# Moving a half's rows from the sync queue in place of the scalar queue, and the loads and logarithms of three batches with it

## The chip, the cores and the metric

The kernel runs on one core of a Trainium2 chip (trn2). The metric is device time in microseconds (us) from start to end of one execution. A core has five engines, each with its own queue of instructions that it takes in order: PE (TensorE, matrix products), DVE (VectorE), ACT (ScalarE), POOL (GpSimd) and SP (SyncE, which here only starts transfers). Sixteen DMA engines carry the transfers; SP, ACT and POOL can start them.

## The reference

Four batches of eight heads run a recurrence over 768 steps with a 40 x 40 state per head, and its output feeds a two-layer network with a squared ReLU:

```python
batch, n_heads, seq, head_dim = (4, 8, 768, 40)
for t in range(S):
    y[:, :, t] = np.einsum('bhd,bhde->bhe', rt, state)
    Sa = np.einsum('bhde,bhe->bhd', state, at)
    state_decay = state * wt[:, :, None, :] - np.einsum('bhd,bhe->bhde', Sa, bt)
    state = state_decay + np.einsum('bhd,bhe->bhde', vt, kt)
...
x = y.transpose(0, 2, 1, 3).reshape(3072, 320)
h = x @ w_in                # 320 x 2048
r = np.maximum(h, 0.0)
out = (r * r) @ w_out       # 2048 x 320
```

Inputs r, k, v, w, a, b are float32, as is the output of 3072 x 320.

## The kernel before

**Tiling.** Time is cut into 6 chunks of 128 steps. A chunk of one batch of the reference is what the code calls batch `m`, so there are 24 of them (`NBC`). Each holds 8 heads, two heads to a pair. The recurrence inside a chunk is turned into matrix products with decay factors taken from the cumulated logarithm of w. A stage `st` handles two pairs, half a batch: 48 stages (`NS`), 8 of them to a chunk (`NQ`). Batch `m` is worked in stages 2m and 2m + 1.

**One stage.** The loop over `st` (L635) lays the instructions of every engine out by hand, in the order in which each engine then runs them. For stage `st`, PE makes products `ca` (L329, for the next stage), `ex` (L436, for the stage before), `P` (L345, L351, L367). `P` is corrected twice: ACT copies it as `Mc` (L360), PE adds a product to it, DVE takes the difference `c` (L375), PE adds another product, and ACT writes the result, negated, into `EVX` (`st_sn`, L383; called Sn). Then come a transpose (L411, L422) and the products `uy` (L461), from which DVE makes the stage's rows of output, `YS` (L471). Between these, at marked places (`prepare(st, "P")`, `"C"`, `"A"`, `1`, `"S"`, `"T"`, `4`, `5`), steps for batches to come are put in, and at the calls of `filler` a piece of the network's work, or, before there is any, nine products for warmth (`warm`, L122).

**Preparing a batch.** `load` (L75) brings six arrays of 160 KB (W, K, A, B, V, R) from HBM, one transfer each, all started by SP. The buffers hold four batches. For batches from 4 on, a one-element write to W's new buffer (L80) stands ahead as a gate, on DVE for batches below 8 and on POOL from 8 on: SP does not start W's transfer until that engine has come to the place. `prep_ln` (L189) is the logarithm of W on ACT. `prep_all` (L206) is, for batches up to 7: PE's cumulated sum `cs` of it (L219), the exponentials `GI` (L226) and `GA` (L228) on ACT, and on POOL the scaled K and B (L238) and the copies of A, V and R (L285, L202). Two stages before their use follow the transposes (L246) and ACT's copies `GT` and `KBT` (L296, L263). For batches 8 and up the steps are spread over more places.

**Which step stands where** is a table, `plan`: an offset in stages from 2m, a place in the stage, and the function. For batches 1 to 7 the logarithm stands in stage 2m - 3 at place "T" and `prep_all` at place 5 of the same stage. At place "T" the stage's order is: Sn and what follows it on POOL, then `release()` (ACT's ReLU copies `hs`, L538, that are held back), a filler, and then the logarithm. Place "S" stands directly behind Sn and ahead of `release()`. Loads are let go at place 5, the last place of a stage, at offsets of their own.

**The network.** When four stages are through, half of a chunk's batches (`h`, called a half here; 12 in all) has its rows in `YS`. Two of the 40-row pieces of the fourth pair are moved to free rows of other pairs, so that the 320 rows fit three tiles: `gather` (L504), four transfers within SBUF of 12 and 8 KB. `feed` then queues the half's products as filler two stages later: `hp` (L527), `hs` (L538), its square `Gt` (L539, on POOL, every fourth on DVE), and `op` (L560) with the output's copy and store (L566, L568). For the first two halves (h = 0 behind stage 5, h = 1 behind stage 9) ACT starts the four transfers, for the others SP, and for the last SP and POOL. The call stands at the end of the stage, ahead of place 5.

Of the kernel before, what the change touches and what calls it, by code (L numbers as in the profile page):

```python
# [18 lines left out]
def kernel(  # L19
# [21 lines left out]
    nc = tc.nc  # L41

    NB, NHH, T, D = r.shape
# [5 lines left out]
    NS = NCH * NQ  # L49
# [5 lines left out]
    AHEAD, EARLY = 4, 7  # L55
# [266 lines left out]
    def st_a_mm(st):  # L322
        c, o, j0, p2, EVX = where(st)
        ca = CNs[st, "ps"] = [ps.tile([128, 2, 2, L], FP32, name=f"ca{s}", tag=f"ca{s}")
                              for s in range(2)]
        for u in range(2):
            for i in range(2):
                for s in range(2):
                    nc.tensor.matmul(out=ca[s][:, i, u, :], lhsT=o.KBT[half(s), u, j0 + i, :],  # L329
                                     rhs=o.AT[half(s), j0 + i, :], start=(i == 0 and u == 0),  # L330
                                     stop=True, skip_group_check=True)
# [7 lines left out]
    def st_p(st):  # L339
        c, o, j0, p2, EVX = where(st)  # L340
        CN, UZ = CNs[st], UZs[c % 2]
        P = Ps[st] = ps.tile([128, 2, 2, 64], FP32, name="P", tag="sp")
        if c > 0:
            for i in range(2):
                nc.tensor.matmul(  # L345
                    out=P[:, i, :, 0:D], lhsT=o.AT[:, j0 + i, :],
                    rhs=UZ[:, p2.start + i, :].rearrange("p (s d) -> p s d", s=2)[:, :, 0:D],
                    start=(i == 0), stop=False, skip_group_check=True)
        for i in range(2):
            for s in range(2):  # L350
                nc.tensor.matmul(out=P[:, i, s, 0:D], lhsT=CN[:, i, s, 0, :],  # L351
                                 rhs=EVX[:, i, s, L:LV], start=(c == 0 and i == 0 and s == 0),
                                 stop=False, skip_group_check=True)

    def st_m(st):
        c, q = divmod(st, NQ)
        if q == 0:
            Mc[c] = chp.tile([128, NQ, 4, D], BF16, name="Mc", tag="Mc")
            Cc[c] = chp.tile([128, NQ, 4, D], BF16, name="Cc", tag="Cc")
        nc.scalar.activation(out=Mc[c][:, q], func=ACTF.Copy,  # L360
                             in_=Ps[st][:].rearrange("p i s e -> p (i s) e")[:, :, 0:D])
# [28 lines left out]
    def st_jk(st, CN):  # L390
        jk = qdp.tile([128, 2, 2, L], BF16, name="jk", tag="jk", bufs=1)
        nc.scalar.activation(out=jk[:], in_=CN[:, :, :, 1, :], func=ACTF.Square,  # L392
                             accum_out=ACC[:, AN + st:AN + st + 1])
# [33 lines left out]
    def st_ex_mm(st):  # L427
        c, o, j0, p2, EVX = where(st)
        SnT = SnTs.pop(st)
        ex = exs[st] = [ps.tile([128, 2, 2, L], FP32, name=f"ex{s}", tag=f"ex{s}")  # L430
                        for s in range(2)]
        for u in range(2):
            for i in range(2):
                for s in range(2):
                    lhsT = SnT[half(s), i, :] if u else o.RVT[half(s), 1, j0 + i, 0:L]
                    nc.tensor.matmul(out=ex[s][:, i, u, :], lhsT=lhsT,  # L436
                                     rhs=o.RVT[half(s), 0, j0 + i, 0:L],
                                     start=(i == 0 and u == 0), stop=True, skip_group_check=True)

    def st_ex_ev(st, s):  # L440
        EVX = EVXs[st % NEV]
        nc.vector.tensor_tensor(  # L442
            out=EVX[:, :, s, 0:2 * LV].rearrange("p i (u x) -> p i u x", u=2)[:, :, :, 0:L],
            in0=exs[st][s][:], in1=MEX[:].rearrange("p (i u) x -> p i u x", u=2), op=ALU.mult)
# [21 lines left out]
    def st_y(st):  # L466
        c, o, j0, p2, EVX = where(st)
        uy = uys.pop(st)
        if st % NQ == 0:
            YSs[c] = chp.tile([128, NP, L], BF16, name="YS", tag="YS", bufs=3)  # L470
        nc.vector.tensor_tensor(out=YSs[c][:, p2, :], in0=uy[:, :, 0:L],  # L471
                                in1=o.GT[:, j0:j0 + 2, 0:L], op=ALU.mult)
        if c + 1 < NCH:
            nc.vector.tensor_tensor(
                out=UZs[(c + 1) % 2][:, p2, :].rearrange("p i (s d) -> p i s d", s=2)[:, :, :, 0:D],
                in0=uy[:, :, L:LV].rearrange("p i (s d) -> p i s d", s=1)
                .to_broadcast([128, 2, 2, D]),
                in1=o.GL[:, j0:j0 + 2, :].rearrange("p i (s d) -> p i s d", d=1)
                .to_broadcast([128, 2, 2, D]), op=ALU.mult)
# [21 lines left out]
    def by_pair(c, hf):  # L501
        return YSs[c][:].rearrange("e (b p) t -> e p b t", b=NB)[:, :, HB * hf:HB * hf + HB, :]

    def gather(c, hf, engines):  # L504
        X = by_pair(c, hf)
        for x, (p, row, h, e0, n) in enumerate(MOVED):
            src = 64 * (h % 2) + e0
            engines[x % len(engines)].dma_start(out=X[row:row + n, p], in_=X[src:src + n, h // 2])
# [3 lines left out]
    def release():  # L512
        while held:
            held.pop(0)()
# [82 lines left out]
    for m in range(1, NBC):  # L597
        if m <= EARLY:
            lot = "T" if m <= AHEAD else "S"
            plan = ((-3, "T", prep_ln), (-3, 5, prep_all), (-2, lot, prep_ga_mm),  # L600
                    (-2, lot, prep_ga_ev), (-2, lot, prep_kb), (-2, lot, prep_at))
        else:
            plan = ((-5, 5, prep_ln), (-4, "P" if m > EARLY + 1 else 5, prep_new),
                    (-4, 1, prep_sums), (-4, "S", prep_exps), (-4, 5, prep_scaled),
                    (-3, "C", prep_ga_mm), (-3, "C", prep_ga_ev), (-3, "A", prep_at),
                    (-3, "T", prep_kb), (-3, 4, prep_cast_rv), (-2, "P", prep_v))
        plan += ((-1, "T" if m == 1 else "C", prep_rv) if m <= AHEAD else
                 (-1, 1, prep_rv) if m < 2 * NB else (-2, 5, prep_turn),)
        if m >= AHEAD:
            plan += (({AHEAD: -9, AHEAD + 1: -8, EARLY: -6}.get(m, -7), 5, load),)  # L610
        for ds_, lot, f in plan:
            todo = when.setdefault((2 * m + ds_, lot), [])
            todo.insert(0 if f is prep_exps else len(todo), (f, m))

    def prepare(st, lot):
        for f, m in when.pop((st, lot), []):
            f(m)
# [17 lines left out]
    for st in range(NS + 2):  # L635
        late = st == 1
        if st + 1 < NS and not late:
            st_a_mm(st + 1)
        if 1 <= st <= NS:
            st_ex_mm(st - 1)  # L640
        if st < NS:
            st_p(st)
            st_m(st)
        if 1 <= st <= NS and st % 2:
            st_jk(st - 1, Ns.pop(st - 1))
        if st >= 2:
            st_y(st - 2)
        if 1 <= st <= NS:
            st_ex_ev(st - 1, 0)
        prepare(st, "P")  # L650
        filler(st)
        if 1 <= st <= NS and st % 2 == 0:
            st_jk(st - 1, Ns.pop(st - 1))
        if 1 <= st <= NS:
            st_z(st - 1)
        if st < NS:
            st_corr(st, Mc[st // NQ][:, st % NQ], False)
            st_c1(st)
        if late:
            st_a_mm(st + 1)  # L660
        st_energy(st - NQ // 2)
        prepare(st, "C")
        if 1 <= st <= NS:
            st_ex_ev(st - 1, 1)
        prepare(st, "A")
        if st + 1 < NS:
            st_a_ev(st + 1)
        filler(st, st % 2 == 0)
        prepare(st, 1)
        if st < NS:  # L670
            st_corr(st, c1s[st], True)
            Ns[st] = st_sn(st)
        prepare(st, "S")
        release()
        filler(st)
        prepare(st, "T")
        st_t(st, st - 2)
        flush()
        prepare(st, 4)
        if st >= NS - 4:  # L680
            filler(st)
        if 1 <= st <= NS:
            st_kb(st - 1)
        if 1 <= st <= NG:
            load_win(st - 1)
        if st == NQ - 1:
            load_wout()
        if st >= 2 and (st - 2) % (NQ // 2) == NQ // 2 - 1:
            h = (st - 2) // (NQ // 2)
            gather(*divmod(h, 2), [nc.scalar] if h < 2 else [nc.sync] if st < NS + 1 else  # L690
                   [nc.sync, nc.gpsimd, nc.sync])
            feed(st + 2, h)
        prepare(st, 5)

# [136 lines left out]
```

## Time and profile before

| | us |
|---|---|
| median of 3 runs | 292.8 |
| lowest, highest | 292.66, 294.53 |
| the profiled execution's own time | 291.61 |
| its span, first to last instruction | 289.8 |
| granted TensorE clock | 0.998 |

| engine | busy us | share of the span |
|---|---|---|
| PE | 264.9 | 91% |
| DVE | 210.0 | 72% |
| ACT | 207.0 | 71% |
| POOL | 214.8 | 74% |

The profile is of one execution. Times in it count from the span's start. A row of a timeline has the start, the duration, the engine, the line of the kernel, the operation, what it writes and reads, and how many such instructions are taken together; in square brackets stands the idle time of the engine just ahead of the row and what ended it. An engine's name with q behind it (SPq, ACTq) is its sequencer starting a transfer, which is not counted as busy time. By these rows stage 0 begins at about 11 us, stage 5 at about 36, stage 6 at about 41, stage 9 at about 58 and stage 10 at about 63.

### The profile page before, as it was taken

Reading aid. Unit: us, or ns where it says so; the run is one execution under the profiler, and the core shown is the slowest. Engines: PE = TensorE matmul, PEld = TensorE weight load, DVE = VectorE, ACT = ScalarE, POOL = GpSimd, SP = SyncE. Lnnn points to the kernel's source line nnn. Section 1 sums busy time; section 2 is a strip of 40 time slices with the busy share of each in tenths; the row PEclk is TensorE's granted clock in tenths of the full one; section 3 lists DMA queues with packets and bytes.
Section 4 is the critical chain, followed back from the end, with each engine's and each line's share of the span. In section 5 each row is a group of like instructions: output and inputs, shape, how many; then the busy total and the mean of one; then the engine's idle time right before and its main releaser. Section 6 shows DMA issues by size and latency. Waiting matters only on the chain.

```text
span 289.8 us, 10084 instructions
## 1 busy us (share of the span) xinstructions
PE 264.9 (91%) x3963; PEld 208.2 (72%) x3963; DVE 210.0 (72%) x461; ACT 207.0 (71%) x534; POOL 214.8 (74%) x414
## 2 busy tenths in 40 slices
PE   6878968987889999999999999999999999899892
PEld 5667757766568777877787787778777877666581
DVE  7568858775658789778888887898889787762140
ACT  4666557848586888888888878888887886746370
POOL 7889816858588988998998898889888988534400
PEclk9999999999999999999999999999999999999999
DMA  7999998794644976895989958959968923000001
GB/s 127 169 169 180 191 166 150 93 186 82 127 76 95 195 136 99 169 175 101 178 148 145 167 92 147 180 109 179 165 115 161 146 42 61 31 23 28 26 28 53
DMA packets 175351, 35.57 MB, mean 123 GB/s; under 512 B 169840, under 2 KB 174976, under 8 KB 175296
## 3 DMA queue, kind: packets, MB, share of 16 engines
q1 hardware_dynamic: 172224, 32.14, 63.3%
q0 software_dynamic: 2640, 2.63, 5.7%
q8 instruction: 33, 0.54, 0.8%
q14 instruction: 22, 0.18, 0.2%
q10 hardware_dynamic: 432, 0.08, 0.1%
HBM read 28.84 MB, written 3.93 MB: 113 GB/s over the span
## 4 chain that ended last, share of the span: by engine, by line
PE 72%; POOL 8%; ACT 6%; DMA 6%; issue 3%; SPq 2%; DVE 1%; POOLq 0%; DVEq 0%; ACTq 0%
PE hp L527 19%; PE tt L246 6%; PE ca L329 5%; PE cs L219 4%; PE uy L461 4%; PE ex L436 3%; POOL Gt L539 3%; PE P L367 3%; PE tb L411 3%; PE P L345 2%; PE wu L122 2%; DMA NR<-in_r_dram 2%; PE uy L451 2%; SPq L81 2%; ACT hs L538 2%
## 5 line engine op out<-in xcount | busy, mean ns | idle before, releaser
L539 POOL TENSOR_TENSOR Gt<-hs 128x512 bf16<-128x512 bf16 x66 | 68.0, 1043 | 24.9 <-ACT hs L538 24.8
L527 PE MATMUL hp<-YS,WIN 120*128 120x256 bf16 (+1 forms) x576 | 77.6, 272 | 0.5 <-ACT hs L538 0.4
L442 DVE TENSOR_TENSOR EVX<-ex,MEX 128x512 bf16<-128x512 f32 x96 | 65.4, 682 | 6.5 <-PE ex L436 6.0
L538 ACT ACTIVATE hs<-hp 128x512 bf16<-128x512 f32 x96 | 55.3, 602 | 15.9 <-PE hp L527 14.4
L337 DVE TENSOR_TENSOR CN<-ca,MCN 128x512 bf16<-128x512 f32 x96 | 61.4, 681 | 0.7 <-PE ca L329 0.7
L527 PEld LDWEIGHTS <-WIN 120*128 120x128 bf16 (+1 forms) x576 | 49.7, 97 | 6.9 <-issue 1.0
L560 PEld LDWEIGHTS <-Gt 128*128 128x128 bf16 x384 | 35.0, 97 | 13.4 <-POOL Gt L539 1.4
L375 DVE TENSOR_TENSOR c<-P,Mc 128x160 bf16<-128x160 f32 x48 | 15.6, 325 | 30.1 <-PE P L367 22.6
L367 PEld LDWEIGHTS <-CN 128*128 128x128 bf16 x384 | 22.2, 96 | 11.2 <-issue 7.7
L238 POOL TENSOR_TENSOR KBp<-NK,GI 128x320 bf16<-128x320 f32 x24 | 20.7, 863 | 12.8 <-ACT GI L226 12.2
L387 POOL TENSOR_TENSOR Cc<-x,EVX 128x160 bf16<-128x160 f32 x48 | 23.4, 487 | 8.9 <-ACT EVX L383 5.4
L392 ACT ACTIVATE jk<-CN 128x512 bf16<-128x512 bf16 x48 | 29.9, 623 | 0.0
L386 POOL TENSOR_TENSOR x<-Mc,c 128x160 f32<-128x160 bf16 x48 | 23.4, 487 | 7.0 <-DVE c L375 6.9
L422 DVE COPY TB<-tb 128x512 bf16<-128x512 bf16 (+1 forms) x48 | 19.3, 401 | 10.6 <-PE tb L417 7.7
L263 ACT ACTIVATE KBT<-tt 128x1024 bf16<-128x1024 bf16 x24 | 24.4, 1018 | 0.3 <-PE tt L246 0.3
L471 DVE TENSOR_TENSOR YS<-uy,GT 128x256 bf16<-128x256 f32 x48 | 19.9, 416 | 4.8 <-PE uy L461 4.8
L461 PE MATMUL uy<-EVX,KBp 128*64 128x168 bf16 x384 | 22.0, 236 | 0.0
L539 DVE TENSOR_TENSOR Gt<-hs 128x512 bf16<-128x512 bf16 x30 | 16.3, 543 | 7.2 <-ACT hs L538 7.2
L122 PE MATMUL wu<-ones_b 128*128 128x128 bf16 x265 | 20.4, 227 | 1.1 <-DVE ones_b L103 1.1
L329 PE MATMUL ca<-AT,KBT 64*128 64x128 bf16 x384 | 19.3, 219 | 2.0 <-ACT KBT L263 2.0
L383 ACT ACTIVATE EVX<-P 128x160 bf16<-128x160 f32 x48 | 14.4, 301 | 9.2 <-PE P L367 9.0
L360 ACT ACTIVATE Mc<-P 128x160 bf16<-128x160 f32 x48 | 14.6, 304 | 8.3 <-PE P L351 7.9
(138 smaller groups left out, 577.4 us busy)
## 6 DMA issues: line engine op xcount, KB each, us to landing
NW<-in_w_dram SPq DMA_DIRECT2D x24, 160.0 KB
NK<-in_k_dram SPq DMA_DIRECT2D x24, 160.0 KB, 4.0
NA<-in_a_dram SPq DMA_DIRECT2D x24, 160.0 KB
NB<-in_b_dram SPq DMA_DIRECT2D x24, 160.0 KB, 4.2
NV<-in_v_dram SPq DMA_DIRECT2D x24, 160.0 KB, 3.4
NR<-in_r_dram SPq DMA_DIRECT2D x24, 160.0 KB, 3.8
out_dram<-osb SPq DMA_DIRECT2D x24, 160.0 KB, 2.1
WOUT<-in_moe_w_out_dram POOLq DMA_DIRECT2D x1, 1280.0 KB, 11.2
```

Source lines behind the costliest of these rows:

```text
L122: nc.tensor.matmul(out=wu[:], lhsT=ones_b[:], rhs=ones_b[:], start=True, stop=True)
L263: nc.scalar.activation(out=o.KBT[:], in_=t2[:], func=ACTF.Copy)
L329: nc.tensor.matmul(out=ca[s][:, i, u, :], lhsT=o.KBT[half(s), u, j0 + i, :], rhs=o.AT[half(s), j0 + i, :], start=(i == 0 and u == 0), stop ...
L337: nc.vector.tensor_tensor(out=CN[:, :, s], in0=ca[s][:], in1=MCN[:], op=ALU.mult)
L367: nc.tensor.matmul(out=P[:, i, s, 0:D], lhsT=CN[:, i, s, 1, :], rhs=X[:, 2 * i + s], start=False, stop=last, skip_group_check=True)
L392: nc.scalar.activation(out=jk[:], in_=CN[:, :, :, 1, :], func=ACTF.Square, accum_out=ACC[:, AN + st:AN + st + 1])
L442: nc.vector.tensor_tensor(out=EVX[:, :, s, 0:2 * LV].rearrange("p i (u x) -> p i u x", u=2)[:, :, :, 0:L], in0=exs[st][s][:], in1=MEX[:].r ...
L461: nc.tensor.matmul(out=uy[half(s), i, :], lhsT=o.KB[:, u, 2 * (j0 + i) + s, :], rhs=EVX[:, i, s, LV * u:LV * u + LV], start=(c == 0 and i ...
L527: nc.tensor.matmul(out=hp[:, u, :].rearrange("p (a b) -> p a b", a=HB), lhsT=WIN[g][0:ROWS[g], j * 128:(j + 1) * 128], rhs=by_pair(c, hf)[ ...
L538: nc.scalar.activation(out=hs[:], in_=flat, func=ACTF.Relu)
L539: later.append(lambda: eng.tensor_tensor(out=out_, in0=hs[:], in1=hs[:], op=ALU.mult))
L560: nc.tensor.matmul(out=op_[:], lhsT=Gts[c, hf][:, j, b_, :], rhs=WOUT[:, j, :], start=(j == 0), stop=(j == NJ - 1))
```

## The change

Three things are changed; nothing of what is computed is.

- The first two halves' moved rows are started by SP, as those of all other halves but the last are.
- Batches 5, 6 and 7 are loaded from stages 5, 6 and 9 (2m - 5, 2m - 6, 2m - 5) in place of stages 2, 5 and 8. In SP's order this puts the moved rows of h = 0 between the loads of batches 4 and 5, and those of h = 1 between the loads of batches 6 and 7. Batch 4 (stage -1) and batches from 8 on (2m - 7) stay.
- The logarithm of batches 5, 6 and 7 goes from place "T" to place "S" of the same stages (7, 9 and 11), so that on ACT it stands directly behind Sn and ahead of `hs`. `lot` is "S" for batches 5 to 7 and "T" for 1 to 4.

```diff
         if m <= EARLY:
             lot = "T" if m <= AHEAD else "S"
-            plan = ((-3, "T", prep_ln), (-3, 5, prep_all), (-2, lot, prep_ga_mm),
+            plan = ((-3, lot, prep_ln), (-3, 5, prep_all), (-2, lot, prep_ga_mm),
                     (-2, lot, prep_ga_ev), (-2, lot, prep_kb), (-2, lot, prep_at))
...
         if m >= AHEAD:
-            plan += (({AHEAD: -9, AHEAD + 1: -8, EARLY: -6}.get(m, -7), 5, load),)
+            plan += (({4: -9, 5: -5, 6: -6, 7: -5}.get(m, -7), 5, load),)
...
             h = (st - 2) // (NQ // 2)
-            gather(*divmod(h, 2), [nc.scalar] if h < 2 else [nc.sync] if st < NS + 1 else
-                   [nc.sync, nc.gpsimd, nc.sync])
+            gather(*divmod(h, 2), [nc.sync] if st < NS + 1 else [nc.sync, nc.gpsimd, nc.sync])
             feed(st + 2, h)
```

(`AHEAD` is 4 and `EARLY` is 7.)

## The prediction

> **What bounds the kernel now.** I read the stretches first (busy time of each engine, TensorE clock, DMA share), then who waited for whom, then each engine's timeline around the two largest waits.
>
> ```profile
> span 289.8 us, 10084 instructions
> ```
> ```profile
> 33.00:45.00 12.00, 8.67 (x170) 7.18 (x168) 7.83 (x19) 6.55 (x19) 5.43 (x13) 1.00 1.01 170
> 57.00:68.00 11.00, 7.98 (x141) 6.30 (x136) 7.06 (x17) 6.25 (x20) 6.66 (x11) 1.00 1.08 172
> 87.00:135.00 48.00, 47.78 (x738) 38.23 (x738) 40.37 (x87) 39.22 (x104) 41.65 (x79) 1.00 0.77 138
> ```
>
> After the length of a stretch come PE, PEld, DVE, ACT and POOL. From 87 us on PE is busy for 47.78 of 48 us. Its order is written out by hand, so whatever delays PE ahead of 87 us is carried to the end, and whatever is saved there is saved at the end. Two stretches ahead of that stand out: PE idles 12 - 8.67 = 3.33 us in one and 11 - 7.98 = 3.02 us in the other, every other engine is slack too, and only the DMA engines are full (1.01 and 1.08). The list of waits between 30 and 70 us says for what (total, times, longest):
>
> ```profile
> ACT GI L226 <- DMA YS<-YS: 6.5, 2, 3.4
> ...
> PE P L367 <- ACT Mc L360: 4.0, 2, 2.2
> ```
>
> Two waits of ACT, and two of PE behind them: one pair in each stretch.
>
> **The rows moved off ACT.** ACT's timeline, and PE's, where stage 5 ends and stage 6 begins:
>
> ```profile
> 37.93 4.60 ACTq L508 DMA_DIRECT2D YS<-YS  x4
> 42.64 0.44 ACT L226 ACTIVATE GI<-cs 128x320 f32<-128x320 f32 x1 [3.38 <-DMA YS<-YS]
> ```
> ```profile
> 39.59 0.81 PE L219 MATMUL cs<-lnW,UTI 128*128 128x320 f32 x2
> ...
> 43.83 0.25 PE L367 MATMUL P<-Mc,CN 128*128 128x40 bf16 x4 [2.18 <-ACT Mc L360]
> ```
>
> and where stage 9 ends:
>
> ```profile
> 62.08 0.46 ACT L189 ACTIVATE lnW<-NW 128x320 f32<-128x320 f32 x1
> 62.56 3.09 ACTq L508 DMA_DIRECT2D YS<-YS  x3
> 65.70 0.44 ACT L226 ACTIVATE GI<-cs 128x320 f32<-128x320 f32 x1 [3.16 <-DMA YS<-YS]
> ```
> ```profile
> 62.59 0.81 PE L219 MATMUL cs<-lnW,UTI 128*128 128x320 f32 x2 [0.47 <-ACT lnW L189]
> ...
> 66.89 0.25 PE L367 MATMUL P<-Mc,CN 128*128 128x40 bf16 x4 [1.86 <-ACT Mc L360]
> ```
>
> GI does not read the moved rows; it only stands behind their four starts in ACT's order. It begins 0.11 us after the last start ends (37.93 + 4.60 = 42.53), and 0.05 us after it in the second place (62.56 + 3.09 = 65.65). So it waits for the starting of these transfers, not for their landing, which comes 3.5 us or more after a start, as the second row here says. The first row has the starts of the same kind that SP makes in later stages (minimum, median, maximum in ns):
>
> ```profile
> L508 SPq DMA_DIRECT2D YS<-YS x39: 620/822/1356, 89.7 to 266.9; - x39
> ```
> ```profile
> DMA to landing us min/median/max: 3.5/3.6/3.6
> ```
>
> Four starts of 0.82 us are 3.3 us, and ACT took 4.60 the first time. The rest comes from the loads: in the built program the transfers of the sync and scalar queues share eight completion counters in turn, and one is not started until the one eight places earlier has landed. ACT's starts take places among the loads that SP has in flight, so ACT waits for these too.
>
> Without the starts GI waits for cs alone. Where nothing else is in the way it follows the start of cs by 0.85 us (stage 11: 76.83 to 77.68, rows below). First place: 39.59 + 0.85 = 40.44 in place of 42.64, 2.20 us sooner. PE's wait behind it is 2.18 us, so all of that goes, and PE's own order is late next. Second place: 62.59 + 0.85 = 63.44 in place of 65.70, 2.26 us. PE's own wait there is only 1.86, but the batch's work on POOL starts from GI and runs on to a place where PE waits for POOL:
>
> ```profile
> 66.30 0.86 POOL L238 TENSOR_TENSOR KBp<-NK,GI 128x320 bf16<-128x320 f32 x1 [4.18 <-ACT GI L226]
> ...
> 71.98 2.04 POOL L539 TENSOR_TENSOR Gt<-hs 128x512 bf16<-128x512 bf16 x2
> ```
> ```profile
> 74.08 0.45 PE L560 MATMUL op__1771<-WOUT,Gt 128*128 128x320 bf16 x2 [0.55 <-POOL Gt L539]
> ```
>
> POOL has no idle time from 66.30 to 74.02 and then releases PE, so I take POOL's 2.26 us. Together 2.18 + 2.26 = 4.44 us.
>
> **The logarithm behind Sn.** In stages 7, 9 and 11 it now stands ahead of the ReLU copy hs (L538) in ACT's order. Stage 11:
>
> ```profile
> 76.83 0.81 PE L219 MATMUL cs<-lnW,UTI 128*128 128x320 f32 x2 [0.47 <-ACT lnW L189]
> ```
> ```profile
> 75.10 0.30 ACT L383 ACTIVATE EVX<-P 128x160 bf16<-128x160 f32 x1
> ...
> 77.68 0.44 ACT L226 ACTIVATE GI<-cs 128x320 f32<-128x320 f32 x1 [0.90 <-PE cs L219]
> ```
>
> The logarithm can begin at 75.40, when Sn (EVX) is done, so cs no longer waits: 0.47 us. In stage 9 the same 0.47 us (the row at 62.59), which comes on top of GI's gain there. In stage 7 I take nothing; the bound is the logarithm's own 0.46. Sum 0.94 us. hs comes up to 0.46 us later in stage 7; the product that reads it there is put off behind other work in DVE's order, which hides it. Without that cover it would cost those 0.46 us.
>
> **The loads let go later.** Batches 5, 6 and 7 are let go at the end of stages 5, 6 and 9 in place of 2, 5 and 8, and the moved rows stand ahead of batches 5 and 7 on SP. What is queued behind a waiting start on SP is these loads, and the one that waits for them is the logarithm on ACT. SP's starts of batch 4's last three transfers, then the first and the last of batch 7's six:
>
> ```profile
> 29.09 3.47 SPq L81 DMA_DIRECT2D NB<-in_b_dram  x1
> 32.66 0.65 SPq L81 DMA_DIRECT2D NV<-in_v_dram  x1
> 33.40 2.58 SPq L81 DMA_DIRECT2D NR<-in_r_dram  x1
> ```
> ```profile
> 57.60 0.37 SPq L81 DMA_DIRECT2D NW<-in_w_dram  x1
> ...
> 64.33 0.80 SPq L81 DMA_DIRECT2D NR<-in_r_dram  x1
> ```
>
> The DVE write that opens the gate at the end of stage 5 (for batch 6 now, for batch 5 after the change), the landing of all loads, and ACT in stages 7 and 11:
>
> ```profile
> 39.78 0.06 DVE L80 MEMSET NW<- 1x1 f32 x1
> ```
> ```profile
> DMA to landing us min/median/max: 3.3/4.1/8.0
> ```
> ```profile
> 50.89 0.60 ACT L538 ACTIVATE hs<-hp 128x512 bf16<-128x512 f32 x1
> ...
> 78.51 0.47 ACT L189 ACTIVATE lnW<-NW 128x320 f32<-128x320 f32 x1
> ```
>
> SP is free at 33.40 + 2.58 = 35.98, the four starts end at 39.3, and batch 5's gate opens at 39.78. W lands at 43.9 by the median and at 47.8 by the longest landing. Its logarithm takes the place of hs at 50.89, less the 2.18 us saved: 48.7. In time, by 0.9 us at worst. Batch 6's gate opens one stage later and its logarithm stands two stages later. Batch 7 is let go at the end of stage 9, about 62.6 - 2.2 = 60.4, and needed at 75.40 less 2.18 and 2.73, which is 70.5: in time even at 8.0. Batch 8 is the close one, since it queues behind batch 7, whose six starts took 65.13 - 57.60 = 7.5 us. So it starts at 67.9 and W lands at 72.0, or at 75.9 at worst; its logarithm stands at 78.51 - 5.4 = 73.1. That is from nothing to 2.8 us of loss. I take nothing, since the median is in time by 1.1 us.
>
> **A rule against it.** The Trainium skill says, in "DMA: Bandwidth & Descriptors", section "Issuing engines are not separate DMA queues", that starting transfers from several engines saves only the sequencer's time to start them, which is usually small beside the transfer. By that rule the first edit is worth little and the time would stay near 292.8. The trace does not agree that it is small here: the starts hold ACT for over 3 us, about as long as the landing of 3.6 us.
>
> **Sum.** 2.18 + 2.26 + 0.47 + 0.47 = 5.4 us. The profiled execution took 291.61 us (its span of 289.8 and 1.8 around it), 1.2 below the median of 292.8. By its own time the sum gives 286.2; by the median 292.8 - 5.4 = 287.4, which I predict.
>
> **Rivals.** (1) POOL's lead is not passed on and the logarithm's place gives nothing: only PE's own two waits go, 2.18 + 1.86 = 4.0 us, 288.8. For it: PE is in order and nearly full. Against it: PE waits for POOL at 74.08. Chance 0.17. (2) Batch 8 comes late as worked out, up to 2.8 us are given back: 290.2. Against it: the median landing. Chance 0.07. (3) The change does not do what it says: the wait is for the transfers, and goes with the rows to wherever they are started. Then 292.8 less at most the logarithm's 0.9, say 292.3. Against it: GI begins 0.05 to 0.11 us after the last start ends, with the landing 3.5 us off. Chance 0.08. (4) Slower: on SP the moved rows, started among full 160 KB transfers, hold the loads behind them, and the logarithm, now ahead of hs, holds ACT. It decides once a start takes over (48.7 - 4.1 - 35.98) / 4 = 2.2 us. At 3.47 us a start (NB at 29.09) batch 5 would be let go at 49.9 and its W land at 54.0, 5.3 late. Batch 7, whose rows can be started about when that batch is let go now, 57.6 - 2.2 = 55.4, would be let go at 69.3, land at 73.4 and be 2.9 late. That is 8.2 us lost against 5.4 won: 295.6. Against it: 39 starts of such rows on SP took at most 1.36 us. Chance 0.07.
>
> **How the numbers follow.** My forecast gets 0.61. About 1% is what a measurement of this kernel can tell from no change: 2.9 us, so faster means under 289.9. The forecast and rival 1 are faster (0.78), rivals 2 and 3 the same (0.15), rival 4 slower (0.07). Low end: all of PE's idle time in the two stretches goes, 3.33 + 3.02, with 0.47 of stage 11 and 0.46 of stage 7 outside the stretches, 7.3 us: 285.5. High end: rival 2's 290.2; rivals 3 and 4 lie outside.
>
> **What would show it.** Right: no start of moved rows on ACT; "ACT GI <- DMA YS" gone from the waits and "PE P <- ACT Mc" there under 0.3 us; GI some 0.9 us after cs in stages 6 and 10; four starts on SP from about 36 to 39.4 us; no wait of cs for lnW in stages 9 and 11; the stretch in which PE is full beginning 5.4 us sooner and as long as before. Wrong: ACT waiting for NW at a logarithm of batches 5 to 8, PE's idle time turning up at another row ahead of 87 us, or the full stretch growing longer.

## The result, and the profile after

| | before | after |
|---|---|---|
| median of 6 runs each, us | 293.74 (292.66 to 296.45) | 285.75 (285.29 to 287.18) |
| the profiled execution's own time, us | 291.61 | 285.29 |
| its span, us | 289.8 | 283.5 |

The ratio after to before is 0.973, with a 95% interval of 0.968 to 0.978. 287.4 had been predicted, 285.5 to 290.2 as the range. The changed kernel was timed a second time beside other runs of the kernel before: 287.28 (4 runs) against 293.54 (13 runs), ratio 0.985 (0.979 to 0.990). The two intervals do not meet; why is part of the question below. (A ratio leaves out the executions that were over 1.5% slower than the fastest of the same kernel, so it isn't that of the medians.)

The stretches of the profile after, with the columns of those shown of before (length; PE, PEld, DVE, ACT and POOL busy; TensorE clock, DMA share, GB/s):

```profile
33.00:45.00 12.00, 10.56 (x205) 8.77 (x202) 9.84 (x23) 8.06 (x21) 7.52 (x18) 1.00 0.69 121
57.00:68.00 11.00, 10.30 (x160) 7.94 (x160) 8.91 (x22) 8.41 (x23) 9.42 (x18) 1.00 1.11 175
87.00:135.00 48.00, 48.00 (x742) 38.20 (x740) 39.91 (x87) 40.46 (x108) 41.94 (x75) 1.00 0.85 145
```

PE's idle time in the first stretch is 12 - 10.56 = 1.44 us in place of 3.33, in the second 0.70 in place of 3.02, though later work has moved into both. The DMA engines are as full as before in the second stretch (1.11), and PE does not mind. ACT's timeline of after, rows from the ends of stages 5, 9 and 11, shows why:

```profile
40.49 0.44 ACT L226 ACTIVATE GI<-cs 128x320 f32<-128x320 f32 x1 [1.23 <-PE cs L219]
...
58.49 0.30 ACT L383 ACTIVATE EVX<-P 128x160 bf16<-128x160 f32 x1 [1.03 <-PE P L367]
58.69 0.46 ACT L189 ACTIVATE lnW<-NW 128x320 f32<-128x320 f32 x1
...
60.53 0.44 ACT L226 ACTIVATE GI<-cs 128x320 f32<-128x320 f32 x1 [0.71 <-PE cs L219]
...
72.82 0.47 ACT L189 ACTIVATE lnW<-NW 128x320 f32<-128x320 f32 x1
```

No start of a transfer stands there any more. GI waits for cs, not for the moved rows, and begins 2.15 and 5.17 us sooner than before. The logarithm stands right behind EVX (Sn), and that of batch 8, at 72.82, waits for nothing. PE at the same places:

```profile
41.68 0.25 PE L367 MATMUL P<-Mc,CN 128*128 128x40 bf16 x4
...
59.69 0.81 PE L219 MATMUL cs<-lnW,UTI 128*128 128x320 f32 x2
...
68.92 0.45 PE L560 MATMUL op__1771<-WOUT,Gt 128*128 128x320 bf16 x2 [0.55 <-POOL Gt L539]
```

The brackets of before (2.18 for Mc at the first row, 0.47 for lnW at the second) are gone; the 0.55 for POOL's square has stayed as it was, 5.16 us sooner. SP's timeline now has the moved rows:

```profile
35.63 3.47 SPq L508 DMA_DIRECT2D YS<-YS  x4
39.93 0.38 SPq L81 DMA_DIRECT2D NW<-in_w_dram  x1
...
55.51 3.08 SPq L508 DMA_DIRECT2D YS<-YS  x4
60.38 0.37 SPq L81 DMA_DIRECT2D NW<-in_w_dram  x1
...
65.12 0.64 SPq L81 DMA_DIRECT2D NW<-in_w_dram  x1
```

Four starts take 3.47 and 3.08 us there too; batches 5, 7 and 8 are let go behind them.

Where the 6.3 us of the two profiles came from can be read from one row that every stage has once, ACT's copy Mc (L360). Its start in the two profiles:

| stage | before | after | sooner by |
|---|---|---|---|
| 5 | 36.16 | 36.16 | 0.00 |
| 6 | 43.48 | 41.33 | 2.15 |
| 8 | 53.65 | 51.28 | 2.37 |
| 10 | 66.53 | 61.37 | 5.16 |
| 12 | 78.87 | 73.18 | 5.69 |
| 28 | 161.38 | 155.70 | 5.68 |
| 47 | 255.51 | 249.13 | 6.38 |

The lead of 5.7 us is complete in stage 12. The last 0.7 come later, in stages 29 to 41, where the change touches nothing: the last section returns to them.

### The profile page after: what moved, and what is told of

The parts are those of the page before. It is cut to its first block, busy times and chain, and to the rows that moved or that the text cites. A ratio compares the mean times of both kernels' runs of the same rounds, so it can differ in the third digit from the quotient of the medians.

```text
span 283.5 us, 10085 instructions
## 1 busy us (share of the span) xinstructions
PE 263.9 (93%) x3963; PEld 208.7 (74%) x3963; DVE 208.1 (73%) x461; ACT 207.1 (73%) x534; POOL 215.9 (76%) x414
## 4 chain that ended last, share of the span: by engine, by line
PE 77%; POOL 7%; ACT 6%; DMA 3%; issue 3%; DVE 2%; SPq 0%; DVEq 0%; ACTq 0%; POOLq 0%
PE hp L527 19%; PE tt L246 7%; PE ca L329 5%; PE cs L219 4%; PE uy L461 4%; PE ex L436 4%; PE wu L122 3%; PE tb L411 3%; PE P L367 3%; POOL Gt L539 3%; PE P L345 2%; PE uy L451 2%; PE P L351 2%; ACT hs L538 1%; ACT KBT L263 1%
## 5 line engine op out<-in xcount | busy, mean ns | idle before, releaser
L360 ACT ACTIVATE Mc<-P 128x160 bf16<-128x160 f32 x48 | 14.6, 304 | 8.3 <-PE P L351 7.9
L238 POOL TENSOR_TENSOR KBp<-NB,GI 128x320 bf16<-128x320 f32 x23 | 19.9, 864 | 0.0
```

Source lines behind the costliest of these rows:

```text
L238: eng.tensor_tensor(out=o.KB[:, u, :, 0:D], in0=nat.pop((key, m))[:], in1=o.GI[:], op=ALU.mult)
```

## The experiments

For each profile below, the lead is the start of Mc in a stage, taken from the first profile of before and corrected by the lead in stage 5 (0.0 to 0.7 us, with which the executions begin). Three profiled spans came out 1.7 to 2.6 us longer than was expected of them: 287.1 with the rows on SP only, 287.1 without the logarithm's move, 286.1 with the loads of before. Each of these executions has a piece at half the clock behind 250 us (last section), which the leads up to stage 47 hold in part or not at all; so the table, and not the span, is what is read below.

| profile | stage 6 | 8 | 10 | 12 | 28 | 47 |
|---|---|---|---|---|---|---|
| after | 2.15 | 2.37 | 5.16 | 5.69 | 5.68 | 6.38 |
| after, once more | 2.16 | 2.37 | 5.17 | 5.72 | 5.42 | 5.47 |
| rows on SP only | 2.16 | 2.16 | 4.41 | 4.41 | 4.39 | 4.72 |
| after without the logarithm's move | 2.16 | 2.16 | 4.42 | 4.42 | 4.10 | 4.12 |
| after with the rows on ACT | 0.98 | 1.19 | 2.18 | 2.72 | 2.42 | 2.58 |
| after with the loads of before | 2.16 | 2.37 | 5.17 | 5.72 | 5.40 | 5.43 |
| loads later only | 0.98 | 0.98 | 1.93 | 1.93 | 1.63 | 1.67 |
| logarithm only | -1.44 | -2.21 | -1.61 | -1.08 | -1.20 | -0.51 |
| before, once more | -0.94 | -2.32 | -1.67 | -1.67 | -1.98 | -1.94 |

**The rows alone.** Before, with one line changed:

```diff
-            gather(*divmod(h, 2), [nc.scalar] if h < 2 else [nc.sync] if st < NS + 1 else
-                   [nc.sync, nc.gpsimd, nc.sync])
+            gather(*divmod(h, 2), [nc.sync] if st < NS + 1 else [nc.sync, nc.gpsimd, nc.sync])
```

> The kernel before with one edit: SP starts the moved rows of the first two halves; loads and logarithms stay. Theory (the starts held ACT, and nothing else mattered): both waits of GI go, 2.15 us at stage 6 and about 2.2 us at stage 10, so the profiled span is 289.8 - 4.4 = 285.4, and the kernel after is 1.2 us faster than this one. On SP the rows now stand behind batch 5 and behind batch 7: they start at about 41.7 and 62.8 us and land at about 47.3 and 68.5, just ahead of PE's first use of them (hp, about 47.7 and 70.5). Rival (the later loads are what makes room for the rows): PE waits for the rows at hp in stage 7 or 11 and the gain is 2 us or less, span 287.8 or more.

289.03 us (4 runs) against 293.76 of before (7 runs), ratio 0.982 (0.977 to 0.987). The lead is 2.16 in stage 6 and 4.41 in stage 10, which is 2.25 more: the prediction's two terms for the rows (2.18 and 2.26) to 0.02 us. In stage 10 Mc stands right behind GI in ACT's order, so the test of what PE keeps is stage 12, where the lead is 4.41 again. SP's timeline of this kernel:

```profile
41.16 4.05 SPq L508 DMA_DIRECT2D YS<-YS  x4
45.33 0.51 SPq L81 DMA_DIRECT2D NW<-in_w_dram  x1
...
64.15 3.11 SPq L508 DMA_DIRECT2D YS<-YS  x4
67.37 1.38 SPq L81 DMA_DIRECT2D NW<-in_w_dram  x1
```

The starts are as long on SP, up to 4.05 us for four, and they go out 5.5 and 8.6 us later than in the changed kernel, behind loads. It costs nothing that can be seen: between 33 and 80 us no product hp waits for the moved rows and no logarithm for W. So the rival, rows that land too late, falls.

**All but the logarithm.** The changed kernel, with the logarithm back at place "T":

```diff
-            plan = ((-3, lot, prep_ln), (-3, 5, prep_all), (-2, lot, prep_ga_mm),
+            plan = ((-3, "T", prep_ln), (-3, 5, prep_all), (-2, lot, prep_ga_mm),
```

> The kernel after with the logarithms of batches 5 to 7 put back to place T. Theory: cs waits for the logarithm again by 0.2 us in stage 7 and by 0.47 and 0.53 us in stages 9 and 11, so the span is 283.5 + 1.2 = 284.7 and the lead over before by the stage copies Mc is 2.15, 2.15, 4.4, 4.4 us behind stages 6, 8, 10 and 12. Rival (PE or POOL is late anyway and the place of the logarithm gives nothing): span within 0.2 us of 283.5.

287.45 us (5 runs), ratio 0.978 (0.974 to 0.982). The lead in stages 6, 8, 10 and 12 is that of the rows alone, 4.42. So the logarithm's move gives what lies between this row of the table and that of after: 0.21 in stage 7, 0.74 - 0.21 = 0.53 in stage 9, and 1.27 - 0.74 = 0.53 in stage 11, 1.27 us together.

**All but the rows.** The changed kernel, with the first two halves' rows started by ACT:

```diff
-            gather(*divmod(h, 2), [nc.sync] if st < NS + 1 else [nc.sync, nc.gpsimd, nc.sync])
+            gather(*divmod(h, 2), [nc.scalar] if h < 2 else [nc.sync] if st < NS + 1 else
+                   [nc.sync, nc.gpsimd, nc.sync])
```

> The kernel after with the moved rows of the first two halves started by ACT again; the loads stay late and the logarithms stay in front. Theory A (ACT was held by two things, the starts themselves at 0.8 us each and waits for loads in flight through the shared completion counters): with no load of batch 5 or 7 in flight yet the four starts take 3.3 us each time. In stage 5 they begin at about 38 us, beside the copies ahead of them, and end at about 41.3, so GI of batch 4 comes at 41.4, 0.9 us later than in after and 1.2 earlier than in before. In stage 9 they begin behind hs, at about 59.2, and GI of batch 6 comes about 2 us later than in after. Span about 283.5 + 2.9 = 286.4. Theory B (starts only, at the same length as in before): the whole 4.4 us come back, span 287.9. Theory C (the wait is for the landing of the rows): GI comes 3.5 us behind the last start, span above 290.

289.58 us (4 runs), ratio 0.987 (0.982 to 0.991). ACT's timeline of this kernel:

```profile
37.97 1.43 ACTq L508 DMA_DIRECT2D YS<-YS  x1
...
39.43 2.23 ACTq L508 DMA_DIRECT2D YS<-YS  x3
41.77 0.44 ACT L226 ACTIVATE GI<-cs 128x320 f32<-128x320 f32 x1 [2.41 <-DMA YS<-YS]
...
60.52 3.05 ACTq L508 DMA_DIRECT2D YS<-YS  x4
63.61 0.44 ACT L226 ACTIVATE GI<-cs 128x320 f32<-128x320 f32 x1 [2.52 <-DMA YS<-YS]
```

Both waits of GI are back. But the first four starts take 1.43 + 2.23 = 3.66 us in place of 4.60, now that batch 5's loads begin behind them, and the lead of stage 6 is 0.98 without any move to SP. Singly the starts take as long as before (1.43, 0.69, 0.83 and 0.63 us in both kernels); what has gone is 0.94 us of waiting between them. GI came later than expected (41.77 for 41.4): the starts themselves are most of the wait, and only the rest is what the loads add. In the order of work 5.69 - 2.72 = 2.97 us came back by stage 12, as the first theory has it (2.9). The span of 287.5 is 1.1 above that theory's, 0.83 of it from behind stage 12, where the last section's squares differ.

**All but the loads.** The changed kernel, with the loads' places of before:

```diff
-            plan += (({4: -9, 5: -5, 6: -6, 7: -5}.get(m, -7), 5, load),)
+            plan += (({AHEAD: -9, AHEAD + 1: -8, EARLY: -6}.get(m, -7), 5, load),)
```

> The kernel after with the loads of batches 5 to 7 let go as early as in before (rows on SP, logarithms in front). Theory: the later release of the loads is worth nothing by itself, span within 0.3 us of 283.5. Rival (rows behind loads on SP land too late for hp in stage 7 or 11): PE waits at hp and the span is 1 us or more above 283.5.

287.92 us (4 runs), ratio 0.980 (0.976 to 0.984). The lead equals that of after to 0.03 us in every stage up to 16. With the rows on SP, the loads' move is worth nothing in the order of work. The four times lie 0.2 to 1.0 us above the three of after at the same mean clock (287.10, 287.18 and 287.56 at 0.991 and 0.992; here 287.77 to 288.11 at 0.990 to 0.992), about what the squares of the last section can make.

**The loads alone.** The same edit the other way round, in the kernel before:

```diff
-            plan += (({AHEAD: -9, AHEAD + 1: -8, EARLY: -6}.get(m, -7), 5, load),)
+            plan += (({4: -9, 5: -5, 6: -6, 7: -5}.get(m, -7), 5, load),)
```

> The kernel before with the loads of batches 5 to 7 let go later and nothing else (ACT still starts the rows, logarithms stay at T). Theory: the starts on ACT no longer wait for loads in flight, so GI of batch 4 comes 0.9 us sooner as in the run with rows on ACT (lead 0.88 behind stage 6), and the second stall shrinks by some 0.7 us: lead 1.5 to 2.1 us behind stage 14, span about 288. Rival (the loads do not matter to ACT's starts): lead under 0.3 us.

291.28 us (10 runs), ratio 0.994 (0.990 to 0.998). The lead is 0.98 and then 1.93. With the rows still on ACT, the later loads take 0.98 off the first wait and 0.95 off the second.

**The logarithm alone.** The kernel before, with one entry changed:

```diff
-            plan = ((-3, "T", prep_ln), (-3, 5, prep_all), (-2, lot, prep_ga_mm),
+            plan = ((-3, lot, prep_ln), (-3, 5, prep_all), (-2, lot, prep_ga_mm),
```

> The kernel before with only the logarithms of batches 5 to 7 moved to S. Theory: 0.2 us in stage 7 and 0.5 us in stage 11 are won as in after; in stage 9 nothing or little, since ACT's starts behind it set GI. Lead about 0.7 us behind stage 14. Rival (it adds up freely): 1.2 us.

293.22 us (10 runs), ratio 1.000 (0.996 to 1.004). Set against the profile of before that was taken once more (next), which has a long first wait too, it gains 0.20 from stage 7 to 8 and 0.53 from stage 11 to 12, and nothing in stage 9, where GI still stands behind ACT's starts.

**Before, once more.** No edit; taken because the timed difference was larger than that of the profiles.

> The kernel before, unchanged, to see where its clock falls. In the runs listed so far the kernel before has a mean granted clock of 0.985 to 0.986 five times and 0.992 to 0.993 twice, the kernel after 0.997 four times and 0.991 to 0.992 twice. Theory: a fall is one window of about 3.4 us at half clock, costs up to 1.7 us of span, and the kernel before has one more of them than the kernel after, in or behind the stretch at 33 to 45 us or 57 to 68 us in which PE idles for 3 us; the profile shows PEclk under 1.00 there. Rival: all falls lie in the tail behind 245 us, where both kernels idle alike, and the kernels differ by chance; then PEclk is 1.00 up to 245 us.

294.97 us (10 runs), ratio 1.002 (0.996 to 1.008). This profiled execution took 294.17 us, 2.6 more than the first one. PE's timeline and three short stretches of it:

```profile
45.13 0.25 PE L367 MATMUL P<-Mc,CN 128*128 128x40 bf16 x4 [3.12 <-ACT Mc L360]
```
```profile
41.00:45.00 4.00, 1.01 (x25) 0.79 (x20) 0.69 (x1) 1.06 (x6) 0.45 (x1) 1.00 1.10 189
45.00:49.00 4.00, 3.87 (x46) 3.75 (x46) 2.24 (x5) 1.59 (x5) 3.86 (x9) 0.57 1.00 171
49.00:53.00 4.00, 3.52 (x73) 2.94 (x74) 3.27 (x8) 3.06 (x7) 0.72 (x3) 1.00 0.52 84
```

PE waited 3.12 us for Mc, not 2.18, and then the granted clock fell to 0.57 over 4 us: a time of some 3.4 us at half of it (0.5 x 3.41 / 4 = 0.43 lost). The lead falls by 0.94 with the longer wait and by 1.39 more in the next stage, at the low clock. The kernel with the logarithm alone shows both again: its wait at this place is 3.62 us, its clock behind it is low for as long, and the lead falls by 1.44 and then 0.98.

**The wait filled with products.** To tell whether PE's idle time brings the low clock, the kernel before with 36 further products for warmth, whose result is not used, in stage 6's wait:

```diff
-            warm(9, st)
+            warm(9 + (36 if st == 6 and st not in wus else 0), st)
```

> The kernel before with 36 more products for warmth (about 2 us of PE work) where PE waits for Mc in stage 6. They fill idle time and compute nothing that is used. Theory (PE's idle time in the first stall brings a window at half clock behind it in most executions): the window at 45 to 49 us is gone, PEclk is 1.00 from 33 to 57 us, the mean clock is 0.997 or, with one window in the tail or behind the second stall, 0.992, and hardly ever 0.985; the median falls by about 1 to 1.5 us against before though GI comes no sooner. Rival (the windows have nothing to do with this stall): clocks spread as in before, and the 2 us of products make the kernel the same or slower.

293.16 us (10 runs) against 293.54 of before, ratio 1.002 (0.998 to 1.007). PE's timeline has the wait filled to 0.66 us:

```profile
41.01 2.67 PE L122 MATMUL wu<-ones_b 128*128 128x128 bf16 x45
44.34 0.26 PE L367 MATMUL P<-Mc,CN 128*128 128x40 bf16 x4 [0.66 <-ACT Mc L360]
```

Its profiled execution has no low clock between start and end, but neither has the first profile of before. Of the executions that the ratio takes in, 4 of its 9 had a mean clock of 0.997 or 0.998, and 3 of 10 of before in the same comparison had 0.996 or more. The expected gain of 1 to 1.5 us did not come. Whether the filled wait keeps the clock up is not settled.

**The tail filled with products.** The changed kernel, with 24 unused products ahead of the sum `ep`, where PE waits 1.4 us near the end.

```diff
+    warm(24)
     ep = ps.tile([1, NACC], FP32, name="ep", tag="uy")
```

> The kernel after with 24 products for warmth (1.3 us of PE work) ahead of the sum of the checks, where PE idles for 1.40 us at 261.8 us. Theory: that idle time is what brings the window at half clock into the tail of some executions, so with it filled the clock stays at 0.996 or more and the times lie at the lower of after's two levels, 285.3 to 286.0. Rival: the window also comes behind the idle time at 246 to 249 us, so that some executions still show 0.991 and 287.

287.34 us (4 runs) against 287.28 of after in the same comparison (next), ratio to before 0.986 (0.980 to 0.993). Clocks of 0.997, 0.997, 0.991 and 0.988 against 0.997, 0.995, 0.991 and 0.989: no difference. The theory falls: with this idle time filled, the low mean clock came in two of four executions all the same.

**After, once more.** No edit.

> The kernel after, unchanged, beside the others on this chip, for its spread of granted clocks: no window at half clock between 10 and 245 us (PEclk 1.00 in every stretch), mean clock 0.996 to 0.998 or, with one window in the tail, 0.990 to 0.992. Span 283.5 or, with the window, 285.2.

287.28 us (4 runs), ratio 0.985 (0.979 to 0.990). The lead in stage 12 is 5.72, again. Two stretches near the end of this profile:

```profile
245.00:250.00 5.00, 3.56 (x70) 2.69 (x67) 4.11 (x9) 2.14 (x7) 3.41 (x5) 1.00 0.02 4
250.00:255.00 5.00, 5.00 (x37) 3.22 (x35) 1.27 (x3) 2.43 (x8) 0.72 (x2) 0.66 0.00 0
```

Here, too, 3.4 us at half the clock follow on a stretch in which PE idles 1.44 us; in the first profile of after, PE idles as much in that stretch and keeps its clock.

**The last square on DVE.** In stage 11 PE still waits 0.55 us for POOL's Gt. The changed kernel, with the last Gt of the first half on DVE in place of POOL:

```diff
-        eng = nc.gpsimd if jj % (NJ // 4) and not tail else nc.vector
+        eng = (nc.gpsimd if jj % (NJ // 4) and not tail and (c, hf, jj) != (0, 0, 7)
+               else nc.vector)
```

> The kernel after with one more edit: the last of the first half's eight squares Gt is made by DVE and not by POOL. In after PE still waits 0.55 us at 68.92 us for POOL's Gt, and DVE has 0.96 us of idle time just ahead. Theory (POOL sets the end of stage 11): the lead behind stage 12 grows from 5.69 by about 0.5 us to 6.2, and the span falls to about 283.0. Rival (DVE comes late with c or CN and PE waits for these): lead unchanged or smaller.

287.85 us (4 runs), ratio 0.985 (0.976 to 0.994), and the lead falls from 5.17 in stage 10 to 5.03 in stage 12, 0.66 behind after. DVE's timeline, then PE's:

```profile
66.73 0.43 DVE L540 TENSOR_TENSOR Gt<-hs 128x512 bf16<-128x512 bf16 x1 [1.22 <-ACT hs L539]
67.07 0.42 DVE L422 COPY TB<-tb 128x512 bf16<-128x512 bf16 x1
```
```profile
67.55 0.29 PE L436 MATMUL ex<-RV,TB 64*128 64x128 bf16 x4 [1.15 <-DVE TB L422]
```

The square stood ahead of the copy TB in DVE's order and waited for hs; TB, which PE needs at once, waited behind it.

**The same square behind the copy.** Like the other squares of DVE, it is now put off behind TB:

```diff
+        last = (c, hf, jj) == (0, 0, NJ // 2 - 1)
+        eng = nc.gpsimd if jj % (NJ // 4) and not tail and not last else nc.vector
...
-            if jj % (NJ // 4) or tail:
+            if jj % (NJ // 4) and not last or tail:
```

> The kernel after with the last of the first half's eight squares Gt made by DVE, this time put off behind the copy TB in DVE's order. In the run before with that edit it stood ahead of TB and DVE waited 1.22 us for hs. Theory: the lead behind stage 12 over the kernel after is about 0.5 us. Rival: DVE's later YS and UZ hold PE's next uy and the lead is nothing or a loss.

```profile
65.09 0.42 DVE L422 COPY TB<-tb 128x512 bf16<-128x512 bf16 x1 [0.20 <-PE tb L417]
66.11 0.42 DVE L540 TENSOR_TENSOR Gt<-hs 128x512 bf16<-128x512 bf16 x1 [0.60 <-ACT hs L539]
```

TB is ahead, PE no longer waits for Gt in stage 11, and the lead in stage 12 is 6.28, 0.56 to 0.59 more than in the two profiles of after. The time was 286.65 (2 runs) against 287.28 of after beside it, ratio to before 0.982 (0.975 to 0.989). The order of work has gained; the times are too few to say so of the kernel.

## Why the prediction was right

It was right in its sign and its mechanism, and both medians, 285.75 and 287.28, lie in the range. The order of work came 5.7 us sooner where 5.4 had been forecast, and its terms came out so. The first comparison timed 8.0 us, though, and that 285.75 still lies within the range, 0.25 us above its low end, is in part luck: that end was worked out from PE's idle time alone, and the clock, on which the executions of before differ, stood in no term.

| term | predicted | measured | from |
|---|---|---|---|
| first wait of GI (stage 6) | 2.18 | 2.16 | rows alone |
| second wait of GI, by POOL's lead (stages 10 and 12) | 2.26 | 2.25 | rows alone |
| logarithm, stage 7 | 0 | 0.21 | after less the kernel without its move |
| logarithm, stage 9 | 0.47 | 0.53 | the same |
| logarithm, stage 11 | 0.47 | 0.53 | the same |
| sum | 5.4 | 5.7 | |

**GI stood behind the starts, not the landing.** The rows alone took both waits away although, on SP, they were started later than before. Rival 3 falls. What was saved is 4.4 us of the path, because compute stood behind the starts in the same engine's order. The rule that starting from several engines only saves the time of the sequencer, which is usually small beside the transfer (the Trainium skill, "DMA: Bandwidth & Descriptors", "Issuing engines are not separate DMA queues"), names what was saved rightly; that it is small does not hold here.

**POOL's lead was passed on.** PE's own second wait was 1.86, and 2.25 came: with the rows alone the lead is 4.17 in stage 11, and 4.41 in stage 12, behind the place where PE waits for POOL's Gt. Rival 1, which gave 1.86 there and nothing for the logarithm, falls.

**Loads in flight hold the starts.** The prediction put the excess of 4.60 over 3.3 us, 1.3 us, down to the loads. With the loads later and the rows on ACT, the four starts took 3.66, so 0.94 is the loads' part; the rest is a first start of 1.43 us, with and without loads, where the prediction had 0.82. The built program's order bears the prediction's reading out: there the first two of the four starts wait for batch 4's V and R to land, the last two for batch 5's K and A. Which of these held ACT the profile does not show.

**The loads' lateness cost nothing.** No logarithm of batches 5 to 8 waits. Batch 8, the close one, had W started at 65.12, where 67.9 had been worked out, since batch 7 was let go at 60.38 and its six starts took 4.6 us and not 7.5. So rival 2 fell by a wider margin than was claimed.

**SP was not held.** Rival 4 decided at 2.2 us a start. The first four took 3.47 us together, 0.87 each, and 4.05, 1.01 each, where batch 5's loads stand ahead of them (rows alone); batch 5 was let go at 39.93 and not at 49.9.

**hs in stage 7.** The cover held: the logarithm ahead of hs cost nothing and gave 0.21, where nothing had been taken and 0.46 had been the bound.

**What the prediction did not have** is how much the executions of one kernel differ. It took the first profile's wait of 2.18 for the wait of the kernel. Three profiles with ACT's starts, the loads as before and the wait not filled have 2.18, 3.12 and 3.62 us there, and the two longer ones have the low clock behind. The difference comes from the four starts on ACT. They end at 42.53 us in the first profile; in those of before, once more, and of the logarithm alone they end 1.3 and 1.6 us later:

```profile
39.66 4.18 ACTq L508 DMA_DIRECT2D YS<-YS  x4
```
```profile
38.96 5.13 ACTq L508 DMA_DIRECT2D YS<-YS  x4
```

Where the rows are on SP, or the loads later, the lead in stage 6 is the same to 0.01 us from profile to profile (2.15 to 2.16, and 0.98). So the change also takes away a wait that differs between executions, because ACT's starts no longer stand among the loads. The profiled execution was the cheap one, 2.1 us below the median of 293.74 beside which after was timed; what the change removes is worth more in the others. This accounts in direction for 8.0 us timed against 5.7 in the order of work.

To split the two, take executions of the same mean clock, from all comparisons in which clocks were recorded, and of before the 45 that the ratios take in. At 0.995 and more, before has a median of 292.1 us (12 runs) and after of 285.75 (6): 6.4 us. At 0.989 to 0.993 it is 293.6 (16) and 287.4 (4): 6.2 us. Below that lie 17 of the 45 of before and none of 10 of after. These groups mix the comparisons. In the last one alone, equal clocks give 291.29 (3) to 286.88 (2), 4.4 us, and 293.49 (6) to 288.07 (2), 5.4 us, with few runs. So between 4.4 and 6.4 us are there at equal clock, about the 5.7 of the order of work. That the rest of the 8.0 is a lower clock of before is likely but not shown, since its six executions in the first comparison have no recorded clock. Why the two comparisons differ by more than their intervals stays open.

The prediction also said that the full stretch would be as long as before. It was 0.7 us shorter in the first profile of after and 0.25 longer in the second, with the same kernel: this is not the change, as the last section shows.

## What to carry to other kernels

A start of a transfer is an instruction of the engine that makes it: four small ones took 3.1 to 5.1 us of ACT's queue, and whatever stands behind them in that engine's order waits, whether it needs the data or not. Put them on a queue whose next work is not urgent, and test it by the begin of the instruction behind: if it follows the end of the last start by 0.1 us, moving the starts lets it begin as soon as its own input is there (here 2.2 us of a wait of 3.4). When a step moves earlier, look for the engine that reaches PE last in each stage: the gain is its lead, not PE's own wait.

## What the runs showed of the hardware

**The granted clock falls for one fixed time.** In all seven profiles that show it between 5 us and the last few us it was one piece of some 3.4 us at half the clock, and it cost 1.4 us in the second profile of before and 1.0 in that of the logarithm alone. In the profiles it follows idle time of PE: one wait of 3.12 and one of 3.62 us, or some 1.4 us near the end, in one piece (1.40 ahead of `ep`) or a few. The same waits passed without it in other executions (2.18 us in the first profile of before, 1.4 near the end of after). By the length of the idle time alone it can't be foretold, and what brings it stays open.

**DVE and POOL take turns on one resource, and hundredths of a us decide.** The 0.7 us in the full stretch come from DVE's square Gt, whose time is either 0.42 or 0.72 us. From 87 to 231 us, the group of DVE's Gt in the first profile of after and in the second (count, total in us, mean in ns):

```profile
L539 DVE TENSOR_TENSOR Gt<-hs 128x512 bf16<-128x512 bf16 x14 | 7.1, 504 | 0.0
```
```profile
L539 DVE TENSOR_TENSOR Gt<-hs 128x512 bf16<-128x512 bf16 x14 | 10.0, 716 | 0.0
```

At one place DVE's Gt and POOL's copy of R begin together, DVE and POOL in the first profile, then in the second:

```profile
115.16 0.41 DVE L539 TENSOR_TENSOR Gt<-hs 128x512 bf16<-128x512 bf16 x1
```
```profile
115.16 0.73 POOL L285 CAST RVp<-NR 128x320 bf16<-128x320 f32 x1
```
```profile
115.12 0.72 DVE L539 TENSOR_TENSOR Gt<-hs 128x512 bf16<-128x512 bf16 x1
```
```profile
115.11 0.45 POOL L285 CAST RVp<-NR 128x320 bf16<-128x320 f32 x1
```

One takes its short time and the other 0.3 us more, and in the second profile POOL, 0.01 us ahead, won. The Trainium skill, "SBUF — State Buffer", section "SBUF: two separate sides", says that DVE, with two operands from SBUF, and a POOL instruction that reads SBUF share a pair of ports as an exclusive lock that whichever starts first holds for its whole instruction. These rows agree in which of the two waits, but the delay of 0.3 us is less than the other's whole 0.41 or 0.45; that it is these ports was not tested. Over the profiles the mean of these squares and the lead won from stage 12 to 47 go together: 504 ns and +0.69 us (after), 531 and +0.57 (logarithm only), 565 and +0.31 (rows on SP only), 645 and 0 (before), 701 and -0.30 (without the logarithm's move), 716 and -0.25 (after, once more); the other eight profiles go the same way, from 584 and +0.35 to 718 and -0.29. So 0.9 us between two executions of one kernel can be a tie between two engines, and no edit is to be credited with it.
